# Pooled attention by quads: four heads at a time, queries in three blocks of 48, turned in two halves

## The chip, the core and the metric

The kernel runs on one core of a Trainium2 chip. The metric is device microseconds of one launch; three runs of a kernel were timed, and one execution was profiled. TensorE (PE) does matrix products and turns tiles (a matmul with the identity). VectorE (DVE), ScalarE (ACT) and GpSimd (POOL) work on tiles, SyncE (SP) issues most transfers.

## What is computed

Attention in two branches over 4 batches, 8 heads, 576 positions and 64 dimensions, then two dense layers that end in 2304 x 512. The change is in the first branch, in which q, k and v are averaged over four neighbours, so that each head has 144 queries and 144 keys.

```python
Sd = S // factor                      # 576 // 4 = 144
q_d = q.reshape(B, H, Sd, factor, D).mean(axis=3)      # k_d, v_d likewise
out_d = sm_attn(q_d, k_d, v_d)                         # softmax(q k^T / 8) v
out_up = np.repeat(out_d, factor, axis=2)
scores = np.where(np.abs(pos[:, None] - pos[None, :]) < factor, scale * q @ k.T, -1e9)
out = out_up + softmax(scores) @ v                     # the local branch
x = out.transpose(0, 2, 1, 3).reshape(B * S, H * D)
h = x @ w_in;  x = (h * np.cos(h)) @ w_out             # first layer, 512 -> 2048 -> 512
out = ((x @ w1) * (x @ w2) @ w3) @ w_out2              # second layer
```

## The kernel before

The program is a list of jobs, Python generators that ask for an engine, a buffer or a condition. A planner (`run`, L294) keeps a clock for each engine from a table of costs (`cost`, L104) and gives an engine that is free the most urgent job that is ready. What it gives becomes the fixed order of the engine's queue; on the chip, semaphores do the waiting. All instructions go through `issue` (L161), so the profile shows L161 for nearly all of them, and tiles tell them apart.

The stages of TensorE's queue: first products of w3 and w4 (`ps_w`, `w5_job`, 64 matmuls of 512 columns), between which the attention of batches 0 and 1 stands, with matmuls on zeros (`ps_z`, `ps_w<-zeros`) where the planner sees TensorE idle; then the first layer in 96 steps, 12 matmuls `ps_h` and 12 `ps_y` each, between which the attention of batches 2 and 3 stands; then the second layer (`ps_ab`, `ps_o`). I call them the ramp, the middle and the end.

Pooled attention is done by `pair_job` (L507), once for each batch and two heads. Averaged queries and keys (`qkd`) come for batch 0 from the tiles of the local branch, else from a load `qkr<-qk_pool` and two reductions on VectorE. Four matmuls give scores of the two heads (`ps_s`), queries in two blocks of 72, a head to a bank. VectorE takes maxima (`nm`), ScalarE exponentials into `sd`, VectorE sums and division (`sums`); then VectorE (batches 0 and 1) or GpSimd multiplies. Eight transposes of 72 columns turn `sd` (`ps_t<-ident,sd`), ScalarE copies the result to `ptp`, and four matmuls with the pooled values `vd` give the output. These stand behind the next pair's transposes in one bank (`ps_t<-ptp,vd`) or, for the last pair of a batch, in a bank of their own (`ps_p`). ScalarE writes the output to `up`, and VectorE adds it to the local branch's output (`xb<-ps_av,up`). `xs` is the sum as the first layer reads it.

The local branch (`unit_job`, L645, 12 units of 192 positions) has scores `ps_sb`, transposes `ps_tb` and values `ps_av`. Its score matmuls use 64 rows and 64 columns of the array, four beside each other. `pool_v_job` (L464) loads `vr` and makes `vd` from it with two additions on VectorE.

Buffers come from rings (`slots`, L188). `raw`, of two buffers, holds qkr, vr, the local branch's qk of later batches, and batch 0's pooled queries and keys. A load on SP waits in order until its buffer's last reader is done. A tile of w_in is loaded (`raw<-w_in`) and prepared by `w_job` (L338): a pass on ScalarE (`t<-raw`), two on VectorE, a copy on ScalarE (`wi<-t`), a subtraction on VectorE.

Of the kernel before, what the change touches and what calls it, by code (L numbers as in the profile page):

```python
# [11 lines left out]
F32R = mybir.dt.float32r  # L12
# [10 lines left out]
P = 128  # L23
# [27 lines left out]
SLOPE, PER_UNIT = 0, 3  # L51
BY_VE = 2
# [7 lines left out]
TOGETHER, PATIENCE = 4, 6750.0  # L60
# [5 lines left out]
U_WI, U_WO, U_W3 = -5, -1.5, -4.5  # L66
# [13 lines left out]
def fused_kernel(ctx: ExitStack, tc: tile.TileContext, qk_block, v_block, qk_pool, v_pool,  # L80
# [23 lines left out]
    def cost(name, op, out, ins, func):  # L104
# [16 lines left out]
        if op == "transpose":  # L121
            return 109 if out.shape[0] == P else 62
# [10 lines left out]
    class Engine:  # L133
# [3 lines left out]
        def __getattr__(self, op):  # L137
            call = getattr(self.engine, op)

            def issue(*args, **kw):  # L140
# [43 lines left out]
    ident_r = const.tile([P, P], F32R, name="ident_r")  # L184
# [3 lines left out]
    slots = {"t": (tp, 2048, 6), "st": (tp, 4096, 1), "g": (gp, 8 * N1, 3), "c": (gp, 4 * N1, 2), "turns": (gp, 4 * N1, 1),  # L188
             "sc": (ap_, 16 * H * KS // 2, 2), "pt": (ap_, 2048, 2), "vb": (ap_, 2048, 2), "raw": (ap_, 32 * SD, 2), "qkd": (ap_, 8 * SD, 2), "sd": (ap_, 16 * SD, 2), "ptp": (ap_, 16 * SD, 1), "vd": (ap_, 16 * D, 1),
             "up": (ap_, 4 * KC * SD, 2), "x": (xp, 4 * KC * N1, 4), "w": (wp, 4096, 2 * F1)}  # L190
# [147 lines left out]
    def w_job(key, src, ring="w"):  # L338
# [17 lines left out]
        yield from on("ve", lambda: ve.tensor_scalar(out=t, in0=t, scalar1=3, scalar2=None, op0=ALU.logical_shift_left), t)  # L356
        yield from on("ve", lambda: ve.scalar_tensor_tensor(out=t, in0=words[:, :, 0], scalar=29, in1=t, op0=ALU.logical_shift_right, op1=ALU.bitwise_or), t)
# [149 lines left out]
    def pair_job(b, p):  # L507
        early, bias = b < EARLY, b < BIAS
        yield from until(reached("sd", b * KC + p))
        fs = yield from take("sd")  # L510
        count("sd")
        f = buf(fs, "sd", [2, 2, SD])[:QP]
        sums, nms = small(fs, "sums", [2, 2], QP), small(fs, "nm", [2, 2], QP)
        if early:
            yield from until(reached(("pooled", b), UPB))
            qk = pool_qk[b][0][:, p]
        else:
            qs = yield from take("qkd")
            raw_slot = yield from take("raw")
            raw = buf(raw_slot, "qkr", [2, SD, 4])  # L520
            yield from on("sy", lambda: sy.dma_start(out=raw, in_=qk_pool[b, p]))
            qk = buf(qs, "qkd", [2, SD])
            for side in range(2):
                yield from on("ve", lambda: ve.tensor_reduce(out=qk[:, side], in_=raw[:, side], axis=AX.X, op=ALU.add), raw)
            give("raw", raw_slot, "ve")
# [3 lines left out]
        def scores():  # L529

            for c in range(2):
                for r in range(2):
                    rs = slice(r * D, (r + 1) * D)
                    pe.matmul(ps[r][:QP, c * SD:(c + 1) * SD], lhsT=qk[rs, 0, c * QP:(c + 1) * QP], rhs=qk[rs, 1, :], start=True, stop=True)

        yield from on("pe", scores, qk)
        if not early:
            give("qkd", qs, "pe")
        elif p == KC - 1:
            give("raw", pool_qk[b][1], "pe")  # L540
        for r in range(2):
            s, nm = ps[r][:QP, :2 * SD].rearrange("p (c k) -> p c k", c=2), nms[:, r]
# [3 lines left out]
            yield from on("ve", lambda: ve.tensor_tensor(out=f[:, r], in0=s, in1=nm.unsqueeze(2).to_broadcast([QP, 2, SD]), op=ALU.add), nms)  # L546
            give_bank(ns[r], "ve")
        if bias:
            yield from on("ve", lambda: ve.tensor_scalar_mul(nms, nms, SCALE / 16.0), nms)

            def exp():
                for r in range(2):
                    for c in range(2):
                        se.activation(out=f[:, r, c], in_=ps[r][:QP, c * SD:(c + 1) * SD], func=AF.Exp, scale=SCALE / 16.0,
                                      bias=nms[:, r, c:c + 1], accum_out=sums[:, r, c:c + 1])
# [13 lines left out]
        yield from on(each, lambda: by.tensor_tensor(out=f, in0=f, in1=sums.unsqueeze(3).to_broadcast([QP, 2, 2, SD]), op=ALU.mult), sums)  # L569

        yield from until(lambda: not p or (b, p - 1) in with_values)
        before = with_values.pop((b, p - 1)) if p else None
        ns = yield from banks(2)
        psts = [bank(n, "ps_t") for n in ns]

        def turn():
            for r in range(2):
                for kc in range(2):
                    for c in range(2):
                        o = (kc * 2 + c) * QP  # L580
                        pe.transpose(psts[r][:QP, o:o + QP], f[:, r, c, kc * QP:(kc + 1) * QP], ident[:QP, :QP])

        def values(of, pso):
            v, t = of[:2]
            for kc in range(2):
                for r in range(2):
                    pe.matmul(pso[r * D:(r + 1) * D], lhsT=v[:, kc, r * D:(r + 1) * D], rhs=t[:, r, kc * SD:(kc + 1) * SD], start=kc == 0, stop=kc == 1)
            if of[2] is not None:
                give(of[2][0], of[2], "pe")
            give("ptp", of[3], "pe")  # L590

# [4 lines left out]
        if p:  # L596
            pso = psts[0][:, 2 * SD:3 * SD]
            yield from on("pe", lambda: (turn(), values(before, pso)), f, *before[:2])
        else:
            yield from on("pe", turn, f)  # L600
        give("sd", fs, "pe")
        tsl = yield from take("ptp")
        t = buf(tsl, "ptp", [2, 2 * SD])[:QP]
# [659 lines left out]
```

## Time and profile before

| | |
|---|---|
| timed runs | 842.82, 836.79, 836.09 us; median 836.79 |
| profiled execution | 836.09 us, its span 834.2 us |
| busy in the span | PE 824.6, DVE 512.0, ACT 454.3, POOL 331.8 us |
| granted clock of TensorE | 1.00 |
| ramp up to the first ps_y | 0 to 113.98 us |
| middle, first ps_y to first ps_ab | 113.98 to 552.46 us |

A row of the trace in order of time gives the start in us, the duration in us, the engine, the operation, its output and inputs, and how many instructions it merges. A matmul of plain fp32 leaves two records, so four score matmuls show as x8. A transpose leaves one, as does a matmul of the layers. A group's row gives the busy time, the mean ns of one, and the idle time before it with what ended it.

### The profile page before, as it was taken

How to read it: one execution, taken by the hardware profiler on the slowest of the kernel's cores; microseconds unless marked ns; L12 is line 12 of the kernel's file. 1: busy time of each engine (PE TensorE's matmuls, PEld its weight loads, DVE VectorE, ACT ScalarE, POOL GpSimd, SP SyncE). 2: the span in 40 equal slices, each digit the busy share in tenths (PEclk: the TensorE clock that was granted, in tenths of full speed). 3: DMA queues.
4: the chain of work that ended last, by engine and by line, in shares of the span. 5: the costliest groups of instructions: out<-in, count | busy, mean ns of one | idle time of the engine just before them, and what ended most of it. 6: DMA issues, size and time to landing. Idle time of an engine off the chain costs nothing.

```text
span 834.2 us, 15559 instructions
## 1 busy us (share of the span) xinstructions
PE 824.6 (99%) x5957; PEld 747.0 (90%) x5957; DVE 512.0 (61%) x929; ACT 454.3 (54%) x920; POOL 331.8 (40%) x313
## 2 busy tenths in 40 slices
PE   8999999999999999999999999999999999999998
PEld 6455679999999899999999999999998999999997
DVE  6988999985777788377353347224436534463342
ACT  4887889675788578657665566531114311331112
POOL 3121232244364544435543445235336533363332
PEclk9999999999999999999999999999999999999999
DMA  8969992234555662453333197770010500020002
GB/s 276 382 219 340 335 363 93 75 108 145 175 169 170 193 199 66 141 182 114 114 115 114 51 320 274 251 240 14 26 26 13 177 26 26 26 93 23 25 26 76
DMA packets 47626, 120.98 MB, mean 145 GB/s; under 512 B 5504, under 2 KB 9856, under 8 KB 47552
## 3 DMA queue, kind: packets, MB, share of 16 engines
q1 hardware_dynamic: 41648, 111.46, 40.0%
q10 hardware_dynamic: 5904, 8.52, 2.9%
q8 instruction: 47, 0.77, 0.4%
q14 instruction: 27, 0.22, 0.1%
HBM read 92.18 MB, written 27.79 MB: 144 GB/s over the span
## 4 chain that ended last, share of the span: by engine, by line
PE 89%; ACT 4%; DMA 3%; DVE 2%; SPq 1%; issue 1%; ACTq 0%; DVEq 0%
PE ps_y L161 24%; PE ps_h L161 24%; PE ps_ab L161 21%; PE ps_o L161 12%; PE ps_w L161 2%; DMA qk<-qk_block 1%; PE ps_t L161 1%; PE ps_av L161 1%; ACT raw L161 1%; PE ps_sb L161 1%; PE ps_tb L161 1%; ACT w L161 1%; SPq L161 1%; DMA raw<-w_in 1%; PE ps_s L161 1%; ACT sd L161 1%
## 5 line engine op out<-in xcount | busy, mean ns | idle before, releaser
L161 PE MATMUL ps_y<-g,wo 128*128 128x384 f32 x1152 | 223.5, 339 | 0.0
L161 PE MATMUL ps_h<-xs,wi 128*128 128x384 f32 x1152 | 216.2, 335 | 0.6 <-DVE wi L161 0.6
L161 PEld LDWEIGHTS ps_y<-g,wo 128*128 128x128 f32 x1152 | 199.2, 188 | 4.6 <-issue 3.6
L161 PEld LDWEIGHTS ps_h<-xs,wi 128*128 128x128 f32 x1152 | 200.9, 188 | 2.6 <-DVE wi L161 1.3
L161 POOL TENSOR_TENSOR g<-c,g 128x384 fp32r<-128x384 f32 x96 | 110.5, 1151 | 208.9 <-ACT g L161 204.6
L161 PE MATMUL ps_ab<-y,w 128*128 128x384 f32 x1008 | 188.7, 337 | 0.5 <-ACT v L161 0.4
L161 PEld LDWEIGHTS ps_ab<-y,w 128*128 128x128 f32 x1008 | 177.6, 188 | 8.3 <-POOL v L161 1.0
L161 DVE TENSOR_TENSOR v<-v,ps_ab 128x384 f32<-128x384 f32 x168 | 90.8, 552 | 141.4 <-PE ps_ab L161 74.5
L161 ACT ACTIVATE c<-c 128x384 f32<-128x384 f32 x192 | 100.7, 524 | 42.4 <-DVE c L161 37.1
L161 ACT CAST m<-v 128x384 fp32r<-128x384 f32 x48 | 24.7, 514 | 176.3 <-POOL v L161 176.3
L161 PE MATMUL ps_o<-w,m 128*128 128x512 f32 x432 | 110.9, 393 | 0.0
L161 POOL TENSOR_TENSOR v<-v 128x384 f32<-128x384 f32 x48 | 50.5, 1056 | 126.4 <-DVE v L161 126.3
L161 DVE SCALAR_TENSOR_TENSOR c<-turns,ps_h 128x384 f32<-128x384 int32 x96 | 52.6, 548 | 64.7 <-ACT turns L161 59.0
L161 PEld LDWEIGHTS ps_o<-w,m 128*128 128x128 f32 x432 | 80.1, 188 | 12.5
L161 DVE SCALAR_TENSOR_TENSOR c<-c,ps_h 128x384 f32<-128x384 f32 x96 | 52.8, 550 | 55.5 <-ACT c L161 55.2
L161 ACT CAST g<-c 128x384 fp32r<-128x384 f32 x96 | 49.2, 512 | 43.7 <-DVE c L161 35.5
L161 ACT ACTIVATE turns<-ps_h 128x384 int32<-128x384 f32 x96 | 46.7, 486 | 29.5 <-PE ps_h L161 29.0
L161 PE MATMUL ps_w<-w,w 128*128 128x512 f32 x128 | 60.7, 606 | 1.1 <-DVE w L161 1.1
L161 POOL TENSOR_TENSOR m<-v,m 128x384 fp32r<-128x384 f32 x48 | 49.2, 1027 | 23.7 <-ACT m L161 23.7
L161 POOL TENSOR_TENSOR xs<-xb,xs 128x384 fp32r<-128x384 f32 x24 | 27.1, 1130 | 52.3 <-ACT xs L161 52.3
L161 PEld LDWEIGHTS ps_w<-w,w 128*128 128x128 f32 x128 | 22.5, 189 | 23.0 <-issue 21.1
L161 DVE SCALAR_TENSOR_TENSOR t<-raw,t 128x512 int32<-128x512 int32 x48 | 40.5, 854 | 0.3
(97 smaller groups left out, 847.3 us busy)
## 6 DMA issues: line engine op xcount, KB each, us to landing
w_sc<-w SPq DMA_DIRECT2D x56, 256.0 KB, 2.4
w<-w_sc SPq DMA_DIRECT2D x28, 512.0 KB, 4.4
raw<-w SPq DMA_DIRECT2D x24, 512.0 KB, 4.6
qk<-qk_block SPq DMA_DIRECT2D x24, 396.0 KB, 3.4
raw<-w3t SPq DMA_DIRECT2D x16, 512.0 KB, 8.3
raw<-w_in SPq DMA_DIRECT2D x16, 512.0 KB, 8.5
raw<-w_out SPq DMA_DIRECT2D x16, 512.0 KB, 8.7
qkr<-qk_pool SPq DMA_DIRECT2D x12, 576.0 KB, 4.4
```

The lines of the kernel that those rows point to most:

```text
L161: return call(*args, **kw)
```

## The change

`quad_job` takes the place of `pair_job`: two jobs of four heads for each batch instead of four jobs of two. Queries are cut in three blocks of 48, each computed 64 rows wide (the last 16 rows are not used), and two heads stand above each other in the partitions 0 to 63 and 64 to 127 of a bank. A score matmul is thus 64 x 64 by 144. The turning is done in two halves (`kc`), each with six transposes of 112 columns; the second half's copy goes into the `sd` buffer itself. Value matmuls are as before, eight in a run. The loads and reductions of `qkr` are done a head pair at a time into one `qkd` tile. Around it: the multiplication of batch 2 moves from GpSimd to VectorE (`BY_VE`), the number of buffers of some rings changes, the first identity goes into a buffer of the `c` ring, up to two exponentials instead of four are gathered before one is issued (`TOGETHER`), and some urgencies change.

```diff
-SLOPE, PER_UNIT = 0, 3
-BY_VE = 2
+SLOPE, PER_UNIT = 0, 2
+BY_VE = 3
-TOGETHER, PATIENCE = 4, 6750.0
+TOGETHER, PATIENCE = 2, 6750.0
-U_WI, U_WO, U_W3 = -5, -1.5, -4.5
+U_WI, U_WO, U_W3 = -5, -1.5, -2.5
-            return 109 if out.shape[0] == P else 62
+            return 109 if out.shape[0] == P else 96
-    slots = {"t": (tp, 2048, 6), ... "c": (gp, 4 * N1, 2), ...
-             ... "qkd": (ap_, 8 * SD, 2), "sd": (ap_, 16 * SD, 2), ... "vd": (ap_, 16 * D, 1),
-             "up": (ap_, 4 * KC * SD, 2), ...
+    slots = {"t": (tp, 2048, 5), ... "c": (gp, 4 * N1, 3), ...
+             ... "qkd": (ap_, 16 * SD, 1), "sd": (ap_, 24 * SD, 2), ... "vd": (ap_, 16 * D, 2),
+             "up": (ap_, 4 * KC * SD, 1), ...
+        if key[0] in ():
...
-    def pair_job(b, p):
+    def quad_job(b, j):
...
-            for side in range(2):
-                yield from on("ve", lambda: ve.tensor_reduce(out=qk[:, side], in_=raw[:, side], axis=AX.X, op=ALU.add), raw)
-            give("raw", raw_slot, "ve")
+            for h in range(2):
+                raw_slot = yield from take("raw")
+                raw = buf(raw_slot, "qkr", [2, SD, 4])
+                yield from on("sy", lambda: sy.dma_start(out=raw, in_=qk_pool[b, 2 * j + h]))
+                yield from on("ve", lambda: ve.tensor_reduce(out=qk[:, h], in_=raw, axis=AX.X, op=ALU.add), raw)
+                give("raw", raw_slot, "ve")
+        queries = qk.rearrange("p h s k -> p h (s k)")
...
-            for c in range(2):
-                for r in range(2):
-                    rs = slice(r * D, (r + 1) * D)
-                    pe.matmul(ps[r][:QP, c * SD:(c + 1) * SD], lhsT=qk[rs, 0, c * QP:(c + 1) * QP], rhs=qk[rs, 1, :], start=True, stop=True)
+            for c in range(3):
+                for h in range(2):
+                    for r in range(2):
+                        rs = slice(r * D, (r + 1) * D)
+                        pe.matmul(ps[r][h * KS:(h + 1) * KS, c * SD:(c + 1) * SD], lhsT=queries[rs, h, c * QW:c * QW + KS], rhs=qk[rs, h, 1, :], start=True, stop=True)
...
-        def turn():
-            for r in range(2):
-                for kc in range(2):
-                    for c in range(2):
-                        o = (kc * 2 + c) * QP
-                        pe.transpose(psts[r][:QP, o:o + QP], f[:, r, c, kc * QP:(kc + 1) * QP], ident[:QP, :QP])
+        ts, rows = [], KS + QW
+        for kc in range(2):
+            ns = yield from banks(2)
+            psts = [bank(n, "ps_t") for n in ns]
+
+            def turn():
+                for r in range(2):
+                    for c in range(3):
+                        pe.transpose(psts[r][:QP, c * P:c * P + rows], f[:rows, r, c, kc * QP:(kc + 1) * QP], ident[:rows, :rows])
...
+            yield from on("pe", lambda: (turn(), values(before, outs) if joins else None), f, *([v for v, _ in before[0]] + before[1] if joins else []))
+            if kc:
+                t = f.rearrange("p r c k -> p (r c k)")[:QP, :4 * SD].rearrange("p (r h k) -> p r h k", r=2, h=2)
+            else:
+                to = yield from take("ptp")
+                t = buf(to, "ptp", [2, 2, SD])[:QP]
+            ts.append(t)
+            for r in range(2):
+                yield from on("se", lambda: se.copy(t[:, r].rearrange("p h (c q) -> p c h q", c=3), psts[r][:QP, :3 * P].rearrange("p (c h q) -> p c h q", c=3, h=2)[:, :, :, :QW]), psts[r])
...
+                for j in range(2):
+                    Job(at + U_PAIR + SLOPE * j, quad_job(b, j))
                 for p in range(KC):
-                    Job(at + U_PAIR + SLOPE * p, pair_job(b, p))
...
-        Job(20, h_job(W5))
+        Job(W5 + 4, h_job(W5))
...
-                    Job(W5 + first[2] + 0 + 5 * f, w12_job(f))
+                    Job(W5 + first[2] + 0 + 4 * f, w12_job(f))
```

The planner then orders all queues anew. Three places follow as the queues stand, each row one instruction or several alike.

TensorE, batch 0 of the pooled branch in the ramp (`ps_w_...` are the products of w3 and w4, `vd` the pooled values); before:

```order
L161 MATMUL ps_s<-qkd 72x144 x4
L161 MATMUL ps_w_293<-w_275,w_294 128x512
L161 MATMUL ps_vd<-vb,fold 72x512 x3
L161 MATMUL ps_s<-qkd 72x144 x4
L161 MATMUL ps_vd<-vb,fold 72x512 x3
L161 MATMUL ps_w_300<-w_275,w_294 128x512
L161 MATMUL ps_w_303<-w_275,w_294 128x512
L161 MATMUL ps_t<-ident,sd 72x72 x8
L161 MATMUL ps_sb<-qk 64x64 x32
L161 MATMUL ps_w_287<-zeros 128x256 x4
L161 MATMUL ps_t<-ident,sd 72x72 x8
L161 MATMUL ps_t<-ptp,vd 64x144 x4
```

and now:

```order
L161 MATMUL ps_s<-qkd 64x144 x12
L161 MATMUL ps_vd<-vb,fold 72x512 x3
L161 MATMUL ps_w_302<-w_274,w_293 128x512
L161 MATMUL ps_w_286<-zeros 128x256
L161 MATMUL ps_t<-ident,sd 72x112 x6
L161 MATMUL ps_w_286<-zeros 128x256 x6
L161 MATMUL ps_sb<-qk 64x64 x32
L161 MATMUL ps_t<-ident,sd 72x112 x6
L161 MATMUL ps_w_286<-w_447,w_460 128x512
L161 MATMUL ps_w_292<-w_447,w_460 128x512
L161 MATMUL ps_t<-ident,sd 72x112 x6
L161 MATMUL ps_t<-ptp,vd 64x144 x2
```

Two stays of scores of four matmuls became one of twelve for each quad, transposes of 72 columns became ones of 112 in two groups of six, seven matmuls on zeros stand where four stood, and the first quad's values follow the second quad's first half.

VectorE, around the additions for unit 1's output (`xb<-ps_av,up`; the `w_...` rows prepare tiles of w3); before, a piece with the first additions of pooled values:

```order
L161 TENSOR_REDUCE qkd<-qkr 128x144
L161 TENSOR_TENSOR sd<-sd,sums 72x576
L161 TENSOR_REDUCE qkd<-qkr 128x144
L161 SCALAR_TENSOR_TENSOR w_782<-w_782,raw 128x512
L161 TENSOR_TENSOR xb<-ps_av,up 128x192 x2
L161 SCALAR_TENSOR_TENSOR w_826<-w_826,raw 128x512
L161 TENSOR_TENSOR vr<-vr 72x2x256
L161 TENSOR_TENSOR xb<-ps_av,up 128x192 x2
L161 TENSOR_REDUCE nm<-ps_s 72x2 x2
L161 TENSOR_TENSOR vd<-vr 72x256
```

and now, with the additions for batch 1's first two pairs of heads:

```order
L161 TENSOR_TENSOR xb<-ps_av,up 128x192 x2
L161 SCALAR_TENSOR_TENSOR w_774<-w_774,raw 128x512
L161 TENSOR_TENSOR vr<-vr 72x2x256
L161 SCALAR_TENSOR_TENSOR w_787<-w_787,raw 128x512
L161 TENSOR_TENSOR xb<-ps_av,up 128x192 x2
L161 TENSOR_TENSOR vd<-vr 72x256
L161 TENSOR_TENSOR vr<-vr 72x2x256
L161 TENSOR_TENSOR vd<-vr 72x256
L161 TENSOR_TENSOR xb<-ps_av,up 128x192 x2
```

The additions on `vr`, whose buffer the first `qkr` load needs, moved ahead of the reductions on `qkr`, and the first `vd` now stands behind the first additions on the third `ps_av`.

TensorE, before the first matmuls of the first layer; before:

```order
L161 MATMUL ps_av<-pt,vb 64x48 x32
L161 MATMUL ps_w_942<-w_275,w_617 128x512
L161 MATMUL ps_sb<-qk 64x64 x32
L161 MATMUL ps_w_948<-w_275,w_617 128x512
L161 MATMUL ps_w_965<-w_275,w_617 128x512
L161 MATMUL ps_w_976<-w_275,w_617 128x512
L161 MATMUL ps_w_942<-w_434,w_681 128x512
L161 MATMUL ps_w_948<-w_434,w_681 128x512
L161 MATMUL ps_h<-xs,wi 128x384 x12
```

and now:

```order
L161 MATMUL ps_w_286<-w_700,w_724 128x512
L161 MATMUL ps_w_292<-w_700,w_724 128x512
L161 MATMUL ps_w_299<-w_700,w_724 128x512
L161 MATMUL ps_w_302<-w_700,w_724 128x512
L161 MATMUL ps_w_917<-w_243,w_656 128x512
L161 MATMUL ps_w_926<-w_243,w_656 128x512
L161 MATMUL ps_w_930<-w_243,w_656 128x512
L161 MATMUL ps_w_939<-w_243,w_656 128x512
L161 MATMUL ps_s<-qkd 64x144 x12
L161 MATMUL ps_h<-xs,wi 128x384 x12
```

Seven more `ps_w` matmuls of w3 and w4 stand between the third `ps_av` and these rows, so 15 in all and one quad's scores lie between it and the first `ps_h`; the local scores and turned tiles that stood there before come later. On SP, the first `raw<-w_in` comes right behind the first `qkr<-qk_pool` now, and behind the third before.

## Rows read from the trace of the kernel before

**Rows 1.** Stretches: length, busy us per engine (instructions), clock, DMA share, GB/s.

```profile
16.08:113.98 97.90, 95.38 (x858) 54.37 (x857) 87.69 (x175) 78.81 (x194) 22.61 (x15) 1.00 0.91 318
113.98:551.00 437.02, 436.51 (x3530) 423.59 (x3529) 289.21 (x519) 302.65 (x593) 187.05 (x165) 1.00 0.49 160
```

**Rows 2.** TensorE's waits: for what; us in total, times, longest.

```profile
PE ps_t L161 <- DVE sd L161: 1.3, 2, 0.7
...
PE ps_h L161 <- DVE wi L161: 0.6, 1, 0.6
PE ps_s L161 <- ACT up L161: 0.5, 1, 0.5
...
PE ps_p L161 <- ACT ptp L161: 0.3, 1, 0.3
PE ps_s L161 <- DVE xb L161: 0.3, 1, 0.3
```

**Rows 3.** TensorE in order of time: start, duration, operation, output, inputs, records.

```profile
30.17 0.73 PE L161 MATMUL ps_w<-zeros 128*128 128x256 f32 x4
...
156.60 1.16 PE L161 MATMUL ps_sb<-qk 64*64 64x64 f32 x64
157.69 1.83 PE L161 MATMUL ps_y<-g,wo 128*128 128x384 f32 x9
...
179.39 1.04 PE L161 MATMUL ps_tb<-ident,sc 128*128 128x128 f32 x8
180.18 2.35 PE L161 MATMUL ps_y<-g,wo 128*128 128x384 f32 x12
...
192.77 1.72 PE L161 MATMUL ps_y<-g,wo 128*128 128x384 f32 x9
194.43 0.71 PE L161 MATMUL ps_s<-qkd 64*72 64x144 f32 x8
195.07 0.80 PE L161 MATMUL ps_y<-g,wo 128*128 128x384 f32 x3
195.71 2.24 PE L161 MATMUL ps_h<-xs,wi 128*128 128x384 f32 x12
197.79 2.24 PE L161 MATMUL ps_y<-g,wo 128*128 128x384 f32 x12
...
212.69 0.67 PE L161 MATMUL ps_t<-ident,sd 72*72 72x72 f32 x8
213.16 2.33 PE L161 MATMUL ps_y<-g,wo 128*128 128x384 f32 x12
...
218.00 0.71 PE L161 MATMUL ps_t<-ptp,vd 72*64 72x144 f32 x8
218.64 2.37 PE L161 MATMUL ps_y<-g,wo 128*128 128x384 f32 x12
```

**Rows 4.** Weight loads of small score tiles: busy us, mean ns, idle before.

```profile
L161 PEld LDWEIGHTS ps_sb<-qk 64*64 64x64 f32 x768 | 12.4, 134 | 3.5 <-issue 1.9 <-ACT up L161 0.8 <-DVE c L161 0.5
...
L161 PEld LDWEIGHTS ps_s<-qkd 64*72 64x72 f32 x128 | 7.7, 139 | 7.9 <-issue 3.4 <-ACT up L161 1.5 <-ACT pt L161 0.9
```

**Rows 5.** ScalarE's table loads: busy us, mean ns, idle before.

```profile
L161 ACT ACT_TABLE_LOAD x20 | 25.7, 1283 | 1.1 <-PEq L1256 0.8
```

**Rows 6.** Head of the profile's page.

```profile
span 834.2 us, 15559 instructions
```

**Rows 7.** TensorE in order of time, a run of ps_w and what follows.

```profile
36.00 6.28 PE L161 MATMUL ps_w<-w,w 128*128 128x512 f32 x14
42.11 0.67 PE L161 MATMUL ps_t<-ident,sd 72*72 72x72 f32 x8
```

**Rows 8.** Critical chain: start and duration of the first w_in tile's transfer, from its issue.

```profile
62.32 6.68 DMA raw<-w_in
```

**Rows 9.** First pass over that tile on ScalarE, and its first use on TensorE.

```profile
74.30 0.73 ACT L161 ACTIVATE t<-raw 128x512 f32<-128x512 f32 x1
...
80.53 2.18 PE L161 MATMUL ps_h<-xs,wi 128*128 128x384 f32 x11 [0.57 <-DVE wi L161]
```

## What I expect the change to do to the time

> **What bounds the kernel now.** The division of the span into stretches comes first. TensorE is busy for 95.38 of the 97.90 us between 16.08 and 113.98 us, and for 436.51 of 437.02 us from there to 551 [rows 1]. All pooled attention lies in these two stretches, the ramp and the middle. The granted clock is 1.00, that is 2.4 GHz, in both. So the time is the sum of what stands in TensorE's queue plus its few waits. What the change takes off VectorE or ScalarE counts only through those waits. The list of TensorE's waits shows how few they are: 1.3 + 0.6 + 0.3 + 0.3 us in the ramp, 0.5 us later [rows 2]. Last I read TensorE's order in time, for what one inserted piece of attention costs [rows 3]. In such a row the duration of the last matmul is modelled, so I use distances from start to start.
>
> **The change, term by term.** Eight quads replace sixteen pairs. Per batch, 16 score matmuls become 24, 32 transposes become 24, and the 16 value matmuls stay.
>
> *Entering and leaving.* One lone pair of scores sits between a 9-matmul and a 3-matmul piece of ps_y. From 192.77 to 195.71 the twelve ps_y and the scores take 2.94 us; twelve alone take 2.08 (195.71 to 197.79). The insertion costs 0.86 us, of which the scores' own row is 0.64 (194.43 to 195.07) [rows 3]. So each stay of small matmuls costs 0.22 us on top, which I carry to the value matmuls.
>
> *Scores.* Before: 16 x 0.64 + 15 stays x 0.22 (one stay holds two pairs) = 13.5 us. The new scores use quarter arrays (64 rows, 64 columns), as the local scores ps_sb already do: 32 matmuls of 64 columns take 1.09 us (156.60 to 157.69), or 34 ns each [rows 3]. For 144 columns that is 34 x 144/64 = 77 ns; a pair's, two at a time, took 0.64/4 = 160 ns. A quad costs 12 x 0.077 + 0.22 = 1.14 us, eight of them 9.1. **-4.4 us.** Bounds: if quarters gave nothing, 8 x (12 x 0.16 + 0.22) = 17.1 us, or +3.6; I take the quarter rate because ps_sb has the same tile shape and the same placing.
>
> Here a rule speaks against the change. ps_sb's weight loads last 134 ns on 64x64 tiles, against 139 for the pair's 64x72 [rows 4]. The Trainium skill (TensorEngine Tiling (Array Packing), Restrictions under Tile-to-Partition Mapping) says that column tiling disables the fast weight load, which would make quarter loads dearer. The trace shows no such loss, so the sum stays. Were loads of 134 ns done one after another, 24 in a quad would take 3.2 us and the term would be +14 us; but ps_sb's 64 loads stand in 1.09 us.
>
> *Transposes.* Before, eight of 72 columns take 0.47 us (212.69 to 213.16), 59 ns each; eight of 128 columns 0.79 us (179.39 to 180.18), 99 ns each [rows 3]. The new ones have 112 columns and no row of their own. On the line between, 59 + 40 x 40/56 = 88 ns. So 96 x 88 = 8.4 us against 128 x 59 = 7.6. **+0.9 us**; at 59 ns it is -1.9, at 99 ns +2.0.
>
> *Values.* The matmul is the same; four take 0.64 us (218.00 to 218.64) [rows 3]. Sixteen stays become eight: **-1.8 us**. Bounds: -0.9 (half the saved stays come straight behind transposes and gave back less) and -2.8 (the longer stay also saves a drain inside).
>
> *Fillers.* The order's seven matmuls on zeros replace four, which took 0.73 us [rows 3]: 3 x 0.18, **+0.5 us**, or 0 where TensorE would have waited anyway.
>
> *At nothing.* VectorE has 8 instead of 16 chains of maxima, sums and divisions, on 128 instead of 72 partitions, so fewer elements per partition (864 against 2 x 576). Its work falls; it is busy for 87.69 and ScalarE for 78.81 us of the ramp's 97.90 [rows 1], so the relief can only shorten waits. Two more table loads at 1.283 us [rows 5] fall where ScalarE is busy 302.65 of 437.02 us [rows 1]; without that cover they cost 2.6 us. The loads of pooled keys and queries stay twelve of one size. The second half of w3t is asked for two steps later: two of its eight loads move behind the first w_in on SP, and they serve the last eight of 64 ps_w matmuls; w12 is made four steps apart instead of five, and its products are used only after 551 us. With one buffer for up and one for qkd, a batch waits until the last is read; the order of the new kernel puts each such write behind the old reader on TensorE, so I count nothing. If that cover is gone, TensorE waits for one addition and one copy, as it did for up before: 0.5 us [rows 2]. The branch in w_job that no key takes, the moved identity and `W5 + 4`, which is 20 as before, issue nothing.
>
> *Sum.* -4.4 + 0.9 - 1.8 + 0.5 = -4.8 us. Each stretch holds four quads: -2.65 us in the middle, and -2.65 + 0.5 = -2.15 in the ramp, where the fillers are. From the span of 834.2 [rows 6]: 829.4. The profiled execution's own time, 836.09, lies 1.9 above its span: 831.3. The median of before, 836.79, lies 0.7 above that execution; the same for the changed kernel gives **832.0 us**. I leave the waits of 3.0 us as they are; where the four in the ramp go is the rivals' matter.
>
> **The rivals.**
>
> *The first weight tile of the hidden layer comes too late (about 837.5).* The first ps_h moves up in the queue. In the new order 15 ps_w matmuls and one quad's scores stand between the third ps_av and it. A ps_w matmul takes two records at 0.43 us (36.00 to 42.11 holds 14) [rows 7], so that is 15 x 0.87 + 1.1 = 14.2 us. But its tile w_in is queued on SP behind a qkr load, and this waits for VectorE's vd addition, which stands behind the xb additions that need that third ps_av. Before, the issue at 62.32 led to the first ps_h at 80.53, 18.2 us later [rows 8, 9]. The least that these rows allow is 6.68 us of transfer and 6.23 us from ScalarE's first pass (74.30) to ps_h [rows 8, 9], 12.9 us. Two xb additions and vd come on top, three instructions at VectorE's mean in the ramp, 87.69/175 = 0.5 us [rows 1]: 12.9 + 1.5 = 14.4 against 14.2, even. With the whole 18.2 us the wait is 18.2 + 1.5 - 14.2 = 5.5, and the time 832.0 + 5.5 = 837.5. For it: ScalarE takes the first pass over this tile ahead of three ps_w copies that TensorE also needs. Against: before, 5.3 us of the 18.2 lay between landing and the first pass, in ScalarE's older queue.
>
> *Slower than before (about 848.5).* The ramp's four ps_h steps each wait: the second w_in stands on SP behind a second qkr load, the fourth behind a qk load that needs both raw buffers, which the qkr reductions free. If each of three steps loses the 5.5 us above anew, 832.0 + 16.5 = 848.5. It decides from 12.8 us of new waits on (844.8). Against: a wait at the first ps_h also gives the later tiles time.
>
> *More than the sum (about 827.8).* VectorE's relief takes the ramp's four waits, 2.5 us, and the transposes cost 70 ns, -1.7 more: 827.8. For it: all but one of these waits are for VectorE. Against: the chain from one quad's transposes through two ScalarE copies to its last values has only one ps_w between.
>
> *Quarters give nothing (840.0).* Scores at +3.6 instead of -4.4: 832.0 + 8.0. Against: ps_sb.
>
> **How the numbers follow.** Forecast 0.58, late weight tile 0.20, more than the sum 0.11, quarters 0.04, slower 0.07. A measurement of this kernel tells about 1% from no change, 8.4 us: faster means under 828.4, slower over 845.2. Faster takes the third rival and a little of the forecast's lower end, 0.12; slower 0.07; within 1% the rest, 0.81. The range reaches from 827.0, under the third rival, to 840.0, over the late tile and at the quarters.
>
> **What would show it.** Twelve ps_s of a quad start to start in about 0.92 us, six transposes of 112 columns in 0.53, eight values in 1.28; the middle stretch about 2.6 us shorter, with no wait over 0.5 us. The first ps_y then stands near 111.8 instead of 113.98. A wait of TensorE before the first ps_h, or at a ps_w before it that ends with a ScalarE copy, speaks for the late tile. A first ps_y before 109.5 us would mean that the relief of VectorE was worth more than I allow. The forecast is wrong if quarter scores run at 160 ns, or if the ramp's waits grow past 5 us.

## The result, and the profile after

The changed kernel takes 828.51 us (median of five runs, 828.22 to 829.21) against 836.79 for the kernel before on the same chip: a ratio of 0.988, 95% interval 0.985 to 0.991, or -8.3 us (0.990 by the two medians; one run of before took 842.82). Beside other kernels on another occasion it took 829.45 against 837.46 (0.991, 0.988 to 0.994), -8.0 us. I had forecast 832.0, -4.8 us, a range from 827.0, and a change of at most 1% with 0.81. The time lies in the range and the change is about 1%, but it is 1.7 times what I had worked out, and the question of this document is where the rest came from.

The profiled execution took 828.71 us, its span is 827.0, so 7.2 us less than [rows 6]. Its windows, cut at the first ps_y and the first ps_ab of the new kernel (stretch: length, then busy us and instructions of PE, PEld, DVE, ACT and POOL, clock, DMA share, GB/s), answer to [rows 1]:

```profile
16.00:110.72 94.72, 94.05 (x880) 54.65 (x878) 85.57 (x152) 78.64 (x180) 17.74 (x13) 1.00 0.94 321
110.72:545.40 434.68, 434.44 (x3555) 424.48 (x3554) 281.32 (x482) 300.66 (x588) 182.87 (x161) 1.00 0.50 164
```

TensorE still bounds both stretches. The first ps_y stands at 110.72 us instead of 113.98, and the middle takes 434.7 us instead of 438.5. All of TensorE's waits of the new kernel, as [rows 2] had them for before (for what, us in total, times, longest):

```profile
PE ps_z L161 <- POOL zeros L161: 1.2, 1, 1.2
PE ps_w L161 <- DVE w L161: 1.1, 1, 1.1
PE ps_tb L161 <- POOL sc L161: 0.5, 1, 0.5
PE ps_ab L161 <- ACT v L161: 0.3, 2, 0.2
PE ps_t L161 <- ACT ptp L161: 0.2, 1, 0.2
PE ps_p L161 <- ACT sd L161: 0.2, 1, 0.2
```

The first two stand before the first product, and those of ps_ab in the end; both kernels have them. None of the waits in [rows 2] is left; 0.5 + 0.2 + 0.2 us stand in their place. The pieces that I had priced, in TensorE's order of time in the middle (start, duration, what, how many records; two records for a plain matmul, one for a transpose):

```profile
198.76 0.97 PE L161 MATMUL ps_s<-qkd 64*64 64x144 f32 x24
199.66 1.51 PE L161 MATMUL ps_y<-g,wo 128*128 128x384 f32 x7
...
234.28 0.74 PE L161 MATMUL ps_t<-ident,sd 112*72 112x112 f32 x6
234.79 1.30 PE L161 MATMUL ps_y<-g,wo 128*128 128x384 f32 x6
235.92 0.45 PE L161 MATMUL ps_t<-ident,sd 112*72 112x112 f32 x3
236.58 0.48 PE L161 MATMUL ps_t<-ident,sd 112*72 112x112 f32 x3 [0.21 <-ACT ptp L161]
236.83 1.30 PE L161 MATMUL ps_y<-g,wo 128*128 128x384 f32 x6
...
240.06 0.74 PE L161 MATMUL ps_t<-ident,sd 112*72 112x112 f32 x6
240.73 0.47 PE L161 MATMUL ps_t<-ptp,vd 72*64 72x144 f32 x4
...
241.86 1.31 PE L161 MATMUL ps_y<-g,wo 128*128 128x384 f32 x6
```

From start to start: twelve scores 198.76 to 199.66, 0.90 us (expected 0.92); six transposes 234.28 to 234.79, 0.51 (expected 0.53); eight values 240.73 to 241.86, 1.13 (expected 1.28). Six transposes with values behind them take 0.67 (240.06 to 240.73), 0.16 more.

To compare whole kernels I use two numbers from here on. Over all of TensorE's rows from the first ps_w to the end, the **waits** are the idle times that the profile puts before a matmul, and the **work** is the sum of the distances from each matmul's start to the next one's, less these waits:

| kernel | work, us | waits, us |
|---|---|---|
| before, two profiles | 814.5, 815.3 | 3.5, 4.3 |
| changed, two profiles | 808.6, 808.8 | 1.3, 1.9 |

So the work fell by 5.7 to 6.7 us and the waits by 1.6 to 3.0. In the first pair of profiles that is -5.9 - 2.2, and +0.9 because the first ps_w came at 12.84 instead of 11.98: -7.2, the difference of the spans. I don't count that last part as an effect of the change: in all profiles below, of either kernel, the first ps_w lies between 11.6 and 12.9 us. In seven of them it comes before 12.0, and in five of these TensorE then waits 0.7 to 1.5 us between 17 and 21 us.

A wait costs more than its row says. Before's wait of [rows 2] for `up` in the middle:

```profile
223.54 0.46 PE L161 MATMUL ps_s<-qkd 64*72 64x144 f32 x2
224.50 0.71 PE L161 MATMUL ps_s<-qkd 64*72 64x144 f32 x6 [0.49 <-ACT up L161]
225.13 1.15 PE L161 MATMUL ps_y<-g,wo 128*128 128x384 f32 x5
```

A pair's scores take 0.64 us [rows 3]; here they take 1.59 (223.54 to 225.13). The row shows 0.49 of idle time, the loss is 0.95: the rest lies under the modelled end of the matmul ahead. In my two numbers it counts as work.

### The profile page after: what moved, and what is told of

Read it like the earlier page. It is cut to its first block, busy times and chain, and to the rows that moved or that the text cites. A ratio compares the mean times of both kernels' runs of the same rounds, so it can differ in the third digit from the quotient of the medians.

```text
span 827.0 us, 15507 instructions
## 1 busy us (share of the span) xinstructions
PE 819.6 (99%) x5992; PEld 747.3 (90%) x5992; DVE 501.0 (61%) x867; ACT 451.3 (55%) x898; POOL 321.7 (39%) x307
## 4 chain that ended last, share of the span: by engine, by line
PE 93%; ACT 3%; DVE 2%; POOL 2%; issue 1%; POOLq 0%; ACTq 0%; DVEq 0%
PE ps_y L161 25%; PE ps_h L161 24%; PE ps_ab L161 19%; PE ps_o L161 11%; PE ps_w L161 6%; PE ps_sb L161 2%; PE ps_av L161 1%; PE ps_t L161 1%; PE ps_tb L161 1%; POOL y L161 1%; PE ps_s L161 1%; PE ps_z L161 1%; PE ps_vd L161 1%; ACT raw L161 1%; ACT w L161 1%
## 5 line engine op out<-in xcount | busy, mean ns | idle before, releaser
L161 POOL TENSOR_TENSOR g<-c,g 128x384 fp32r<-128x384 f32 x96 | 108.3, 1128 | 209.4 <-ACT g L161 193.3
```

The source lines that it names most:

```text
L161: return call(*args, **kw)
```

## The experiments

Two theories stood from the start. **Work**: what TensorE no longer does gives the time, as I had summed it. **Relief**: VectorE has less to do, and TensorE's waits in the ramp go. The third is **Order**: the five numbers that the change also sets (`PER_UNIT`, `BY_VE`, `TOGETHER`, `U_W3`, the spacing of w12) order the queues otherwise, and with that order the waits go. Each run's ratio is to the kernel before, timed beside it on the same chip.

**Half the rate for the scores.** The scores of the two heads that stand above each other are issued one head after the other, so that only two matmuls should run beside each other.

```diff
-            for c in range(3):
-                for h in range(2):
+            for h in range(2):
+                for c in range(3):
```

> The changed kernel with the twelve score matmuls of a quad in another order: the two heads that stand above each other one after the other, so that only two 64x64 matmuls can run beside each other, not four. Nothing else moves. Theory (four quarter matmuls run at once): twelve take 12 x 0.16 = 1.9 us instead of 0.90, so 8 x 1.0 = 8.2 us more, about 836.7. Rival (the gain comes from fewer stays and waits, not from the rate of the scores): within 1 us of the changed kernel, 828.5.

Measured: 830.55 us, 0.992 (0.990 to 0.994), 1.1 us over the changed kernel beside it. Neither theory's number. A quad's scores follow; the first two rows hold what had started by 199.285 and by 199.655 us, the third holds all:

```profile
198.98 0.59 PE L161 MATMUL ps_s<-qkd 64*64 64x144 f32 x6
198.98 0.95 PE L161 MATMUL ps_s<-qkd 64*64 64x144 f32 x18
198.98 1.26 PE L161 MATMUL ps_s<-qkd 64*64 64x144 f32 x24
200.17 1.15 PE L161 MATMUL ps_y<-g,wo 128*128 128x384 f32 x5
```

1.19 us instead of 0.90, in all eight quads, 2.4 us in sum (work 810.8; only 1.1 of it shows in the time, because this execution's waits were 0.5 us shorter and its first ps_w 0.4 us earlier than those of the changed kernel beside it). But the edit did not hold the matmuls to two at a time. The first head's matmuls start alone, six records in 0.31 us; then the second head's start among them, twelve records in the next 0.36 us; the last six come alone again. Half of the records still ran as before, so this run gives no price for two at a time.

**Wide score tiles in the kernel before.** Its four matmuls are 128 queries wide instead of 72; the rest of the columns is not used.

```diff
-pe.matmul(ps[r][:QP, c * SD:(c + 1) * SD], lhsT=qk[rs, 0, c * QP:(c + 1) * QP], rhs=qk[rs, 1, :], start=True, stop=True)
+pe.matmul(ps[r][:, c * SD:(c + 1) * SD], lhsT=qk.rearrange("p s k -> p (s k)")[rs, c * QP:c * QP + P], rhs=qk[rs, 1, :], start=True, stop=True)
```

> The kernel before with its score matmuls 128 queries wide instead of 72 (the 56 more are not used); all else in its order. In the changed kernel twelve matmuls of 64 columns take 0.90 us, or 1.19 when only two can run beside each other: 75 and 99 ns each against 160 ns for a pair's of 72. Theory (a tile wider than 64 columns is priced as a whole width of the array): four still take 0.64 us and the time is that of before, 837. Rival (each column of the tile costs): four take 0.64 x 128/72 = 1.14 us, and with 16 such runs the time is 8 us longer, 845.

Measured: 837.76 us once, before 837.09 (median of seven). One piece:

```profile
196.80 0.76 PE L161 MATMUL ps_s<-qkd 64*128 64x144 f32 x8
197.49 0.80 PE L161 MATMUL ps_y<-g,wo 128*128 128x384 f32 x3
```

Four take 0.69 us at 128 columns against 0.64 at 72: 78% more columns cost 7% more. The first theory holds. What 64 columns change shows in the pace at which the records of a stay start. Three steps of it, in before, in this run and in the changed kernel (started by 194.85, 197.26 and 199.17 us):

```profile
194.43 0.59 PE L161 MATMUL ps_s<-qkd 64*72 64x144 f32 x6
196.80 0.64 PE L161 MATMUL ps_s<-qkd 64*128 64x144 f32 x6
198.76 0.60 PE L161 MATMUL ps_s<-qkd 64*64 64x144 f32 x12
```

The fourth step makes the first two rows 0.71 [rows 3] and 0.76 us long, and three more make the last one 0.97. So a step takes 0.12 us (122 ns by the starts of the single records) at 72, 128 and 64 columns alike; but two records start in it at 72 and 128 columns, and four at 64. It is not the narrower tile that is faster: four of them run beside each other. What is left of a stay's row is entering and leaving: 0.64 = 4 x 0.122 + 0.15 for a pair, 0.90 = 6 x 0.122 + 0.17 for a quad. A pair's 160 ns a matmul are thus 122 of pace and 38 of this.

**Values in two stays.** In four of the eight runs of values (one per batch) the order six transposes, eight values becomes three, four, three, four.

```diff
...
-            yield from on("pe", lambda: (turn(), values(before, outs) if joins else None), f, *([v for v, _ in before[0]] + before[1] if joins else []))
+            def turn_and_values():
+                held_back[0] = []
+                turn()
+                values(before, outs)
+                calls, held_back[0] = held_back[0], None
+                for n in (0, 1, 2, 6, 7, 8, 9, 3, 4, 5, 10, 11, 12, 13):
+                    go, args, kw = calls[n]
+                    go(*args, **kw)
...
+            yield from on("pe", turn_and_values if joins else turn, f, *([v for v, _ in before[0]] + before[1] if joins else []))
```

`held_back` collects TensorE's calls, which the loop then issues in the new order.

> The changed kernel, in which the six transposes and eight value matmuls that stand behind each other are cut into three transposes, four value matmuls, three transposes, four value matmuls, in 4 of the 8 runs of values (one for each batch): 4 more stays of values. By the price of my prediction, 0.22 us each, TensorE's work grows by 0.9 us. By the issue distances of the two traces (four values alone 0.64 us, eight 1.13; transposes ahead of values 0.13 to 0.16 longer than ahead of a layer) a stay of values costs 0.15 + 0.15 + about 0.1 = 0.4, and the work grows by 1.2 to 1.7 us. If a stay of values cost nothing, 828.5 stays.

Measured: 831.46 us, 0.993 (0.990 to 0.996). One of the four places:

```profile
339.83 0.45 PE L623 MATMUL ps_t<-ident,sd 112*72 112x112 f32 x3
340.21 0.47 PE L623 MATMUL ps_t<-ptp,vd 72*64 72x144 f32 x4
...
340.86 0.48 PE L623 MATMUL ps_t<-ident,sd 112*72 112x112 f32 x3
341.27 0.47 PE L623 MATMUL ps_t<-ptp,vd 72*64 72x144 f32 x4
...
341.91 2.35 PE L146 MATMUL ps_y<-g,wo 128*128 128x384 f32 x12
```

339.83 to 341.91 is 2.08 us; uncut it was 1.80 (240.06 to 241.86 above, and the same in this place). One more stay of values costs 0.28 us, a little over my 0.22, and four of them 1.1. The other part of the 2 us is waits, 3.4 us against 1.3 and 1.9: two of them (0.9 and 0.6, at 18 and 21 us) stand before the first value matmul, so this edit did not make them; with the first ps_w at 11.96 they are like those of the other early starts.

**VectorE's load back.** The maxima of batches 0 and 1 are taken twice.

```diff
-            yield from on("ve", lambda: ve.tensor_reduce(out=nm, in_=s, axis=AX.X, op=ALU.max, negate=True), ps[r])
+            yield from on("ve", lambda: ve.tensor_reduce(out=nm, in_=s, axis=AX.X, op=ALU.max, negate=True) and bias and ve.engine.tensor_reduce(out=nm, in_=s, axis=AX.X, op=ALU.max, negate=True), ps[r])
```

`bias` is true in batches 0 and 1.

> The changed kernel with each of the 8 maxima of batches 0 and 1 taken twice on VectorE: about 8 x 0.51 = 4.1 us more of VectorE's work in the ramp (85.6 to 89.7 us, above the 87.7 of before), all of it on the chain from a quad's scores to its transposes. All queues keep their order. Theory A (VectorE's relief removed TensorE's waits in the ramp): waits of TensorE for VectorE come back to 2 us or more and the time is 830.5 or more. Theory B (the new order of the queues removed them): they stay under 1 us in sum, and the time within 0.8 us of 828.5.

Measured: 834.48 us, 0.997 (0.995 to 0.998), 5.0 us over the changed kernel. Its waits are 6.6 us; the longest came at the first transposes:

```profile
30.14 0.45 PE L161 MATMUL ps_t<-ident,sd 112*72 112x112 f32 x3
32.37 0.48 PE L161 MATMUL ps_t<-ident,sd 112*72 112x112 f32 x3 [1.77 <-DVE vd L161]
32.62 0.96 PE L161 MATMUL ps_w<-zeros 128*128 128x256 f32 x6
```

That is as Relief has it: VectorE's work ahead of these transposes holds TensorE up. The eight added maxima take 0.60 us each, 4.8 us, and about as much is lost.

**VectorE's load taken off before.** The reverse, in before's order, for batches 0 and 1 only.

```diff
...
-            yield from on("ve", lambda: ve.tensor_reduce(out=nm, in_=s, axis=AX.X, op=ALU.max, negate=True), ps[r])
+            yield from on("ve", lambda: ve.tensor_reduce(out=nm, in_=s, axis=AX.X, op=ALU.max, negate=True, real=(lambda call: call(out=nm, in_=s[:, :, :QP], axis=AX.X, op=ALU.max, negate=True)) if bias else None), ps[r])
...
-        yield from on(each, lambda: by.tensor_tensor(out=f, in0=f, in1=sums.unsqueeze(3).to_broadcast([QP, 2, 2, SD]), op=ALU.mult), sums)
+        yield from on(each, lambda: by.tensor_tensor(out=f, in0=f, in1=sums.unsqueeze(3).to_broadcast([QP, 2, 2, SD]), op=ALU.mult, real=(lambda call: call(out=f[:, :, :, :QP], in0=f[:, :, :, :QP], in1=sums.unsqueeze(3).to_broadcast([QP, 2, 2, QP]), op=ALU.mult)) if bias else None), sums)
```

The planner counts the call as it was; `real` is what is issued in its place.

> The kernel before, with all queues in its order, but in batches 0 and 1 the maxima take only half of the keys and the multiplication only half of the columns (the other halves are left out): VectorE's work in the ramp falls by about 8 x (2 x 0.15 + 0.37) = 5.4 us, most of it on the chains from scores to transposes. Theory A (VectorE's relief removes TensorE's waits): the ramp's five waits fall from 2.43 us to under 1, the stretch from the first ps_w to the first ps_y from 102.0 to 100.5 or less, the time 1.5 us or more under before. Theory B (the order does it): the waits stay at 2 us or more, the time within 0.8 us of before.

Measured: 836.56 us, 0.999 (0.997 to 1.0005). VectorE's ramp:

```profile
16.08:113.98 97.90, 95.08 (x854) 54.03 (x854) 83.43 (x174) 77.47 (x192) 21.64 (x15) 1.00 0.92 311
```

83.43 us busy against 87.69 [rows 1], twice the relief that the change brought (to 85.57, in a ramp 3 us shorter). The two waits for sd shrank from 1.3 to 0.5 us, and others stood up:

```profile
PE ps_h L162 <- DVE wi L162: 0.6, 1, 0.6
PE ps_t L162 <- DVE sd L570: 0.5, 2, 0.3
PE ps_s L162 <- DVE qkd L162: 0.4, 1, 0.4
...
```

In sum 3.4 us with the smaller ones, as before. Relief alone falls as the cause: the waits for VectorE's `sd` get shorter, but in before's order others take their place, and the time does not move by more than 0.3%. The two runs together fit an order that is fixed ahead: what comes late against it is lost, what comes early gains little. They do not say whether the new order could do without the 2.1 us that VectorE was relieved of; load_back put more than twice as much back.

**The numbers alone, and the quads alone.** Before's pairs with the five new numbers; the changed kernel with the five old ones. The planner orders each anew.

```diff
-SLOPE, PER_UNIT = 0, 3
-BY_VE = 2
-TOGETHER, PATIENCE = 4, 6750.0
-U_WI, U_WO, U_W3 = -5, -1.5, -4.5
-                    Job(W5 + first[2] + 0 + 5 * f, w12_job(f))
+SLOPE, PER_UNIT = 0, 2
+BY_VE = 3
+TOGETHER, PATIENCE = 2, 6750.0
+U_WI, U_WO, U_W3 = -5, -1.5, -2.5
+                    Job(W5 + first[2] + 0 + 4 * f, w12_job(f))
```

> The kernel before, pairs of heads as they were, with the changed kernel's numbers alone: PER_UNIT 2, BY_VE 3, TOGETHER 2, U_W3 -2.5, w12 four steps apart. The planner orders the queues anew. If the quads carry the gain: within 1 us of before. If the order that the numbers give removed the waits: 2 us or more faster than before, with ramp waits under 1 us.

> The changed kernel's quads with before's numbers: PER_UNIT 3, BY_VE 2, TOGETHER 4, U_W3 -4.5, w12 five steps apart. The planner orders the queues anew. If the quads carry the gain, TensorE's work falls as in the changed kernel: 829 to 830, with ramp waits of about 1 us. If the numbers removed the waits, the ramp's waits stay at 2.4 us and the time is 830.5 to 832.

Measured: numbers alone 836.58 us, 0.999 (0.997 to 1.001), nothing; waits 5.0 us, in an execution of 839.05 us that is 2.5 over the median. Quads alone 831.54 us, 0.993 (0.991 to 0.995), -5.4 us. Their longest waits:

```profile
PE ps_sb L161 <- ACT sd L161: 0.7, 1, 0.7
PE ps_s L161 <- DVE qkd L161: 0.7, 1, 0.7
PE ps_h L161 <- ACT sd L161: 0.5, 1, 0.5
...
```

With the work at 810.4 us (4.1 to 4.9 less than before) and the waits at 3.4 (3.5 and 4.3 before). This is the kernel that I had summed up: the work down by 4.8, the waits as they were, 832.0. The five numbers give the other 2 to 3 us, and only with the quads. That is near the noise: the six runs took 830.8 to 832.6 us, the nine of the changed kernel on two occasions 828.2 to 831.2, and the interval here overlaps both of the changed kernel's.

**One number back at a time,** in the changed kernel: `PER_UNIT` and `U_W3`, `BY_VE`, `TOGETHER`, the spacing of w12. Each edit is a line of the diff above, reversed.

> The changed kernel with two of its five numbers back: PER_UNIT 3 and U_W3 -4.5, which set when the local branch's units and the second half of w3t come. All five numbers back cost 2.1 us (831.5 against 829.4). If these two are what matters, about 831.5; if not, 829.4.

> The changed kernel with one of its five numbers back: batch 2 is multiplied on GpSimd again (BY_VE 2). The multiplication of 864 elements on GpSimd lies on the chain from scores to transposes in the middle. If this number is what matters: about 831.5, with new waits of TensorE behind 110 us; if not, 829.4.

> The changed kernel with one of its five numbers back: up to four exponentials are gathered before one is issued (TOGETHER 4), so that ScalarE changes its table less often. If each number is tuned to the others, as the two runs before suggest (BY_VE back: +3.3 us, the urgencies back: +1.7), this one costs 1 to 3 us as well, in waits of TensorE; if this one doesn't matter: 828.5 to 829.5.

> The changed kernel with one of its five numbers back: w12 made five steps apart instead of four. Its products are used behind 551 us only, and its making takes ScalarE, VectorE and GpSimd in the middle. I counted it as nothing: 828.5 to 829.5. If the order that it gives matters: 1 to 3 us more, in waits behind 180 us.

| put back | time, us | ratio (95%) | over 829.45 | work, waits |
|---|---|---|---|---|
| PER_UNIT, U_W3 | 831.19 | 0.993 (0.991 to 0.995) | +1.7 | 809.9, 2.7 |
| BY_VE | 832.79 | 0.995 (0.994 to 0.997) | +3.3 | 810.9, 4.6 |
| TOGETHER | 832.54 | 0.995 (0.993 to 0.997) | +3.1 | 810.2, 4.4 |
| w12 | 830.46 | 0.993 (0.991 to 0.994) | +1.0 | 808.9, 2.0 |
| all five | 831.54 | 0.993 (0.991 to 0.995) | +2.1 | 810.4, 3.4 |

The single steps add up to 9 us and all together cost 2: these are no prices of the numbers, each is the price of an order that no longer fits. That of w12 is within what two occasions of one kernel differ by (828.5 and 829.4), and all these intervals overlap or touch the changed kernel's (0.988 to 0.994). With BY_VE back the largest loss is not near the multiplications, which stand on GpSimd between 216 and 314 us; it stands at 423 us, where ScalarE reads the four `ps_y` banks out (`yt`):

```profile
420.97 1.21 PE L161 MATMUL ps_y<-g,wo 128*128 128x384 f32 x6
423.40 0.79 PE L161 MATMUL ps_y<-g,wo 128*128 128x384 f32 x3 [1.23 <-ACT yt L161]
425.26 1.31 PE L161 MATMUL ps_y<-g,wo 128*128 128x384 f32 x3 [1.07 <-ACT yt L161]
426.37 3.33 PE L161 MATMUL ps_h<-xs,wi 128*128 128x384 f32 x12
429.54 1.72 PE L161 MATMUL ps_y<-g,wo 128*128 128x384 f32 x9
```

**Without the fillers.** The seven matmuls on zeros are planned but not issued.

```diff
...
-            pe.matmul(ps[:, :WARM], lhsT=zr[:, :P], rhs=zr, start=alone, stop=alone)
+            if alone:
+                pe.matmul(ps[:, :WARM], lhsT=zr[:, :P], rhs=zr, start=alone, stop=alone)
+            else:
+                pe.planned_only(ps[:, :WARM], zr[:, :P], zr)
```

`planned_only` counts the time in the plan and issues nothing.

> The changed kernel without the seven matmuls on zeros in the ps_w banks, all else in its order. They took 1.40 us of TensorE's queue. If TensorE would have waited there anyway (for the divided sd and the second unit's scores), the time is that of the changed kernel, 828.5 to 829.5, and waits of about 1.4 us stand at the rows behind; if they delay the ramp, as I counted, the first ps_y comes 0.5 to 1.4 us earlier and the time is 827 to 828.

Measured: 829.46 us, 0.990 (0.987 to 0.993), the time of the changed kernel. Waits of 0.5 and 0.8 us stand where they were:

```profile
30.48 0.33 PE L168 MATMUL ps_sb<-qk 64*64 64x64 f32 x2 [0.49 <-ACT sd L168]
31.57 1.16 PE L168 MATMUL ps_sb<-qk 64*64 64x64 f32 x62 [0.76 <-ACT sd L168]
```

The fillers cost nothing.

**Each kernel once more.**

> The changed kernel once more, beside the others on one chip: 828.5 us, TensorE's waits behind the first product near 0.9 us, the first product between 12.0 and 12.9 us.

> The kernel before once more, for how far two profiled executions of one kernel differ in TensorE's waits: a span of 834 to 836 us, waits of 2 to 4 us in sum, TensorE's work within 0.3 us of the first profile.

Measured: 829.45 us for the changed kernel (four runs), 837.97 once for before, with the work and waits of the table above. Work repeats to 0.8 us, where I had expected 0.3, and waits to 0.8. Of before's waits [rows 2] those of ps_t for sd (once), of ps_p for ptp and of ps_s for xb came again; the one of ps_h for wi and that for `up` did not, and others stood up. So a part of the waits belongs to the execution, not to the kernel.

## Why the prediction was right or wrong

**What bounds.** Right: TensorE is busy for 94.05 of 94.72 and 434.44 of 434.68 us. The middle became 3.8 us shorter where I expected 2.6, and the first ps_y came at 110.72 where I expected 111.8; before 109.5, where I had set the mark for VectorE's relief, it did not come. That mark was no good one: with the quads alone the first ps_y came at 108.91, with 2.1 us of waits in the ramp, because 64 `ps_av` and 16 `ps_p` records that stand in the ramp of the changed kernel come behind it there. In the two kernels themselves the same work of attention stands on either side of it.

**Scores.** Right in size and in the reason, wrong in the bound. A quad took 0.90 us for the 0.92 expected, and four records start in each step of 0.122 us where two did. But I bounded the case that they don't with 160 ns a matmul, a pair's row divided by four, and 38 of these are entering and leaving, which a longer stay pays once. At 122 ns the bound is 8 x (12 x 0.122 + 0.16 + 0.22) = 14.8 us, +1.3 instead of +3.6, and the rival of 840.0 would have been one of 837.7. The pace is also less than half of the gain: by the rows the scores fell from 13.5 to 8 x (0.90 + 0.22) = 9.0 us, of which 64 - 48 = 16 steps are 2.0 us; the other 2.6 come from eight stays in place of fifteen. The Trainium skill (TensorEngine Tiling (Array Packing), Available Configurations) lists, for 64 rows, four tiles 64 columns wide and two that are 128 wide, and none between; the traces agree, with four records a step at 64 columns and two at 72 and 128. The rule that I weighed, that column tiling disables the fast weight load, again showed nothing in the time.

**Transposes.** Right: 85 ns each, 88 expected.

**Values.** Mis-sized. I took -1.8 for eight stays at 0.22. Eight in a run take 1.13 us where two runs of four take 1.28, so 8 x 0.15 = 1.2 more were saved inside, as the outer bound of -2.8 had it, for which I had no row; the extra stay that was put in cost 0.28. By that the term is -2.2, by both together up to -3.0.

**Fillers.** 0 instead of +0.5: TensorE would have waited.

**Work in sum.** -4.8 forecast; -4.1 to -4.9 with the quads alone, in which some waits hide, and -5.7 to -6.7 in the changed kernel. The terms as measured, -4.6 for scores, +0.6 for transposes (96 x 85 ns), -2.2 to -3.0 for values and 0 for fillers, are -6.2 to -7.0. So the sum was short by 1 to 2 us, mostly in values and fillers. The middle says the same: of its 3.8 us the rows show only 0.3 less waits (0.5 to 0.2), so about 3.6 are work, where I had 2.65.

**The step that failed** is "I leave the waits of 3.0 us as they are", and behind it the list of edits counted at nothing. The five numbers had no term in my sum; BY_VE and PER_UNIT I did not even name there. They order the queues anew, and with the quads that order took the waits from 3.4 us to 1.3 and 1.9. The work fell by another 1.6 to 1.8. Both kernels issue the same 5992 TensorE records, so I take that for the part of waits under modelled ends; about 1 us of it stands in distances right beside a wait, and where the rest comes from is not shown. Quads with the old numbers gave 831.5, where I had said 832.0, in part by luck, since the terms saved more than I had summed and this order lost about as much; the changed kernel has 828.5. I had looked at what each edit costs on its engine, and an edit of the order costs nothing there. Waits 1.6 to 3.0 us shorter and a sum 1 to 2 us short make up the 3.5 us that I was off.

**The rivals.** The late weight tile did not come: w_in was issued at 57.30 us and passed by ScalarE at 62.72, and its last subtraction ended at 67.4, before the quad's scores in front of it:

```profile
62.72 0.67 ACT L161 ACTIVATE t<-raw 128x512 f32<-128x512 f32 x1
...
66.72 0.68 DVE L161 TENSOR_TENSOR wi<-t,wi 128x512 fp32r<-128x512 f32 x1
...
69.04 2.37 PE L161 MATMUL ps_h<-xs,wi 128*128 128x384 f32 x12
```

11.7 us from issue to use and no wait, less than the 12.9 that I had taken as the least [rows 8, 9]. The first part was shorter: 5.4 us from the issue to ScalarE's pass, where I had 6.68 for the transfer alone; the second was 6.3, as before. (Also, the first ps_h of before stood at 79.56, one matmul ahead of the 80.53 that I used.) "More than the sum" had nearly the right time, 827.8, and the ramp's waits right, with a cause that alone doesn't do it and transposes at 70 ns that took 85: luck in part. Taking work from VectorE in before's order did not remove them (before_relieved), and the number that cost most when it was put back, BY_VE, is one that gives VectorE more work, not less. That VectorE's load can hold TensorE up, load_back shows; taken alone it is not what held TensorE up before. Slower: no new chain of waits came (its mark of 844.8 should have been 836.79 + 8.4 = 845.2).

**What stays open.** Whether the new order would remove the waits without the quads' relief of VectorE is not shown; no run has the one without the other, since the numbers alone with pairs give another order. And which wait each number removes in the changed kernel can't be told one by one, since every number moves the whole order.

## What to carry to other kernels

Where a planner or a table fixes the order, a change of its numbers is a term of the sum too: it can take at most all waits of the critical engine with what hides under them (3.5 us in the rows here, and 0.2 to 0.5 us more under each of three waits that I followed), and it can add as much (single numbers put back cost 1.0 to 3.3 us). Test such a change in two parts, the new work under the old numbers and the old work under the new ones; here the one gave -5.4, the other nothing, and both -8. For plain fp32 products of 64 rows, cut the stationary side to 64 columns and alternate the two column halves, so that four run beside each other where 72 columns let two, and gather them in few stays: a stay cost about 0.16 us in its own row and 0.22 around it.

## What the runs showed of the hardware

- Plain fp32 matmuls of 64 rows and 144 columns out started in steps of 0.122 us a record (two records a matmul) at 64, 72 and 128 stationary columns alike; four records started in a step at 64 columns, two at 72 and 128. With entering and leaving that was 75 ns a matmul in a run of twelve at 64 columns, and 160 and 173 ns in runs of four at 72 and 128.
- An idle time of TensorE in a row is less than what was lost: 0.49 us shown, 0.95 lost at 223.54 in before; 0.21 shown, 0.40 lost at 235.92 in the changed kernel (0.91 for six transposes instead of 0.51); 1.77 shown, 1.97 lost at 30.14 in load_back (2.48 instead of 0.51).
- With BY_VE back TensorE's clock fell behind two waits, 1.23 and 1.07 us, that ended at 423.40 and 425.26. The three ps_y behind the second took 1.11 us (425.26 to 426.37) instead of 0.52, and the twelve ps_h then 3.17 us (426.37 to 429.54) instead of 2.08. The granted clock (the third number from the end of a window's row) was 0.66 over four us, which is 1.2 GHz for two thirds of them and 2.4 for the rest:

```profile
426.00:430.00 4.00, 4.00 (x17) 4.00 (x17) 0.00 (x0) 0.77 (x2) 1.01 (x1) 0.66 0.30 112
430.00:434.00 4.00, 4.00 (x25) 4.00 (x24) 1.11 (x2) 2.09 (x6) 1.32 (x2) 1.00 0.16 58
```

That is 1.7 us more than the waits themselves. In the next four us the clock was back at 1.00. Behind load_back's single wait of 1.77 us it stayed at 1.00 (32 to 36 us).
